# Turning batch 1's q on VectorE instead of TensorE in a fused attention and FFN kernel

## The chip, the cores and the metric

The kernel runs on one core of one Trainium2 chip. The metric is the device time of one execution in microseconds; lower is better. The time before is the median of three runs.

## The reference

Pooled attention over 8 batches, 8 heads, 576 positions and 64 channels per head, then a feed-forward network on the result, all in fp32:

```
k_p, v_p = mean of k, v over groups of 8 positions        # 72 keys per head
attn     = softmax(q k_p^T / 8) v_p                       # [8, 8, 576, 64]
x        = attn as [4608, 512]
h        = x @ w_in                                       # [4608, 2048]
g        = h + sin(alpha h)^2 / alpha
out      = g @ w_out                                      # [4608, 512]
```

## The kernel before

**Two halves.** The first half computes g and writes it to DRAM (`g_bridge`); the second reads it back and multiplies by w_out. Both matrix products are done by Strassen-like schemes with seven products of blocks in place of eight (names such as `a11`, `as1`, `as4` and `bt` are blocks and their sums or differences). The change is in the first half, near its beginning.

**Units and slots.** The first half runs over units u of 512 tokens (`hidden`, from line 839). A unit has four groups J of columns of w_in, and each group seven slots: slot 7J + k holds one block product of four matmuls (`product`, line 863, matmul at line 871), which the trace shows as eight instructions. The products k = 0 to 6 of a group go through four PSUM banks b1, b6, b5, b7; VectorE adds what comes out of them into the tile `h` (line 842), ScalarE takes sines and squares (lines 1056 and 1063), `finish` adds the squares (line 1111), and `store_g` sends the group to DRAM. w_in is loaded in four parts, one for each J (`load_w_in_part`), and each part is combined by four additions (`combine_w_in`, line 692) into the blocks that the seven products need.

**Attention beside the products.** While unit u runs, the attention of batch b = u + 1 is worked out in between: `carry` (line 1233) puts each of its steps into the list of a slot with `at(slot, step, ...)`, and `hidden` calls the list at that slot. The order in which the program issues instructions is the order on each engine; there is no other scheduler, and every queue (SP's DMA queue too) works in that order. The first batch is done before unit 0, in `first_batch`. Unit 0 is the case changed here; there batch 1's attention runs beside the products of unit 0.

The steps of batch 1 are:

- `load_k`, `load_q`, `load_v`: DMAs on SP's queue; GpSimd pools k and v by additions (`pool_rows`, line 132). The tiles `kvin` for k and v are two, used in turn.
- `pairs_q`: ScalarE copies q so that two heads lie side by side (line 98).
- `q_t(i)`: TensorE transposes four pairs of heads of one block of 128 positions (line 294; five blocks, the last with 64 positions), and ScalarE or VectorE copies the result out of PSUM (line 295) to the tile that the scores read.
- `k_t`: TensorE turns the pooled keys (line 283), VectorE copies them (line 284).
- `two_scores(j)`: the scores of two blocks (line 322), with `shifts` on VectorE (lines 345, 346) that take the maximum away; it uses banks 5, 6, 7 and one that the FFN's rotation leaves free.
- `exp` (ScalarE), `norm` (sums on VectorE, the product on GpSimd, line 379), `turn` (VectorE turns blocks of 32x32 of the weights into the tile `tr`, lines 508 to 518), `move` (16 DMAs from `tr` to `aM`, line 528), `all_values` (TensorE, lines 617 and 630), `to_x` (ScalarE writes the next unit's x).

**Batches 2 to 7 already differ from batch 1.** Their q is turned by `turn_q` (line 220): VectorE turns 32x32 blocks into `tr` (lines 233 and 238), and 16 DMAs put the blocks where the scores read them (line 248). `columns` (line 297) and `value_parts` (line 547) know both layouts. Batch 2's q is turned and moved in slots 23 to 26 of unit 0.

**Other lines named below.** Line 837 (`sums_of_x`) is VectorE's difference of blocks of x; line 466 is the norm of batch 0's last 64 rows; line 217 sums batch 0's v, line 1157 is warm-up work before the inputs are there.

Of the kernel before, what the change touches and what calls it, by code (L numbers as in the profile page):

```python
# [19 lines left out]
P = 128  # L20
# [20 lines left out]
class Kernel:  # L41
# [46 lines left out]
    def pairs_q(self, b, tiles):  # L88

        nc = self.nc  # L90
        if 0 in tiles:
            self.raw = self.q_views(self.qm[b])
            self.qm[b] = self.q_tile(1)
        x = self.qm[b][:].rearrange("p (t h e d) -> p t e h d", t=5, e=2, d=self.D)
        for t in tiles:
            n = P if t < 4 else 64
            raw = self.raw[0][:, :, t, :] if t < 4 else self.raw[1]
            nc.scalar.copy(out=x[:n, t], in_=raw.rearrange("p (e h) d -> p e h d", e=2))
# [35 lines left out]
    def load_v(self, b, parts=(0, 1, 2)):  # L134
# [6 lines left out]
        for s in range(2):  # L141
            if s in parts:
                nc.sync.dma_start(out=t[64 * s:64 * s + 64],
                                  in_=self.v[b, 4 * s:4 * s + 4, 0:4 * P, :].rearrange("h (p t) d -> p h (t d)", t=POOL))
# [74 lines left out]

    def turn_q(self, b, part):  # L220
# [42 lines left out]
    def attention(self, b):  # L263
# [22 lines left out]
        def q_t(i, copy=nc.scalar.copy):  # L286

            n = rows[i]
            x = self.qm[b][:n].rearrange("p (t hp x) -> p t hp x", t=5, hp=NP)[:, i]
            if b not in self.qt:  # L290
                self.qt[b] = self.qt_view(self.q_tile(0))
            ps = self.abank([P, NP, P])
            for hp in range(NP):
                nc.tensor.transpose(ps[:, hp, :n], x[:, hp], self.ident[:n, :n])  # L294
            copy(out=self.qt_tiles(b)[:, i, :, :n], in_=ps[:, :, :n])

        def columns(hp, i):

            if b < 2:
# [230 lines left out]
        def to_x(ps, hp, t0, m, s0=0):  # L530

            while s0 < m:
# [5 lines left out]
                if t0 and b > 1:  # L538
# [8 lines left out]
        def value_parts(hp, rest):  # L547
# [14 lines left out]
            order = lambda x: x.rearrange("p a (t i) -> p t a i", i=32) if b == 1 else x  # L562
            at = lambda r, n, h: order(self.aM[r:r + n, :, 128 * h:128 * h + 128])
# [74 lines left out]
        return SimpleNamespace(**{f.__name__: f for f in (k_t, q_t, products, score, two_scores, two_shifts, exp, norm, new_a, turn, move, values, values_rest, all_values,  # L638
# [497 lines left out]
    def first_batch(self):  # L1136
# [96 lines left out]
    def carry(self, u):  # L1233
# [6 lines left out]
        if u == 0:  # L1240
# [509 lines left out]
```

## Time and profile before

| what | us |
|---|---|
| median of three runs | 898.12 (897.59 to 899.59) |
| the profiled execution | 897.74 |
| span of the profiled execution, first to last instruction | 895.9 |
| TensorE busy in it | 890.3 |
| VectorE busy | 682.0 |
| ScalarE busy | 458.7 |
| GpSimd busy | 243.5 |

The profile's times are microseconds from the start of the span. Rows of the chain give start, length and what ran. Rows of the timeline give start, busy time, engine, line, operation, tiles, shapes and count, and in brackets how long the engine was idle before and what ended that. Rows that begin with a line number give minimum, median and maximum duration in ns. SPq is the queue that issues DMAs; a DMA's issue is shown there, not its landing. A row of the table by windows gives the stretch, its length, the busy time (and count) of PE, PEld, DVE, ACT and POOL, TensorE's granted clock, the DMA engines' mean busy share, and GB/s. PE is TensorE, PEld its weight loads, DVE VectorE, ACT ScalarE, POOL GpSimd. Every instruction of an fp32 product appears twice.

### The profile page before, as it was taken

What the parts mean: (1) busy time and instruction counts of PE and PEld (TensorE: products, weight loads), DVE (VectorE), ACT (ScalarE), POOL (GpSimd) and SP (SyncE); (2) the same over time, 40 slices, a digit from 0 to 9 for tenths busy, and PEclk for the clock granted to TensorE, in tenths of its full rate; (3) what the DMA queues carried; (4) which work ended last, traced back from release to release, by engine and by line L of the source; (5) the groups of instructions that cost most, each with busy time, mean ns of one, the idle gap of its engine ahead of it and who ended that gap; (6) DMA issues with size and microseconds to landing.
All of it is one profiled execution on the core that took longest, in us unless ns stands there. A gap on an engine that the chain in (4) does not pass through costs nothing.

```text
span 895.9 us, 16414 instructions
## 1 busy us (share of the span) xinstructions
PE 890.3 (99%) x6310; PEld 814.6 (91%) x6310; DVE 682.0 (76%) x924; ACT 458.7 (51%) x1069; POOL 243.5 (27%) x265
## 2 busy tenths in 40 slices
PE   9999999999999999999999999999999999999998
PEld 6787888888888888888888999999999999999998
DVE  7876767768576675765677889898897896996885
ACT  5687877878878797787776711111111211111111
POOL 6699444624356342524523000000000000000000
PEclk9999999999999999999999999999999999999999
DMA  9958677576765857348126243716435355164002
GB/s 256 252 159 240 193 188 221 154 210 199 188 201 162 229 182 190 131 126 317 54 107 217 104 179 104 231 36 218 117 103 159 92 158 160 36 194 142 18 18 53
DMA packets 119533, 141.03 MB, mean 157 GB/s; under 512 B 45776, under 2 KB 86496, under 8 KB 119456
## 3 DMA queue, kind: packets, MB, share of 16 engines
q1 hardware_dynamic: 116288, 137.39, 52.3%
q10 hardware_dynamic: 3168, 2.61, 1.0%
q8 instruction: 50, 0.82, 0.4%
q14 instruction: 27, 0.22, 0.1%
HBM read 75.37 MB, written 47.19 MB: 137 GB/s over the span
## 4 chain that ended last, share of the span: by engine, by line
PE 98%; DMA 1%; SPq 0%; issue 0%; DVE 0%; ACT 0%
PE PS L871 43%; PE PS L1420 43%; PE PS L1089 6%; PE PS L322 2%; PE PS L617 2%; PE PS L630 1%; DMA h<-in_v_dram 1%; PE PS L575 0%; PE PS L294 0%; PE PS L283 0%; PE PS L573 0%; SPq L169 0%; PE PS L483 0%; PE PS L429 0%; PE PS L217 0%; PE PS L491 0%
## 5 line engine op out<-in xcount | busy, mean ns | idle before, releaser
L871 PE MATMUL PS<-home,a 128*128 128x256 f32 x1072 | 255.7, 381 | 0.1
L871 PEld LDWEIGHTS PS<-home,a 128*128 128x128 f32 x1072 | 197.1, 190 | 29.6 <-issue 4.6
L871 PE MATMUL PS<-home,as 128*128 128x256 f32 x688 | 167.9, 382 | 0.0
L871 PEld LDWEIGHTS PS<-home,as 128*128 128x128 f32 x688 | 124.8, 190 | 16.6 <-ACT PS L843 1.2
L1420 PE MATMUL PS<-s,wb 128*128 128x192 f32 x672 | 116.2, 326 | 0.0
L1063 ACT ACTIVATE s<-s,c 128x256 f32<-128x256 f32 (+1 forms) x236 | 115.5, 556 | 0.0
L1420 PEld LDWEIGHTS PS<-s,wb 128*128 128x128 f32 x672 | 110.4, 190 | 0.1
L842 DVE TENSOR_TENSOR h<-PS,p 128x512 f32<-128x512 f32 x72 | 49.3, 684 | 56.5 <-PE PS L871 34.0
L1591 ACT COPY PS<-PS 128x192 f32<-128x192 f32 x42 | 12.7, 303 | 145.9 <-PE PS L1420 129.7
L1420 PE MATMUL PS<-r,wb 128*128 128x192 f32 x432 | 79.0, 326 | 0.0
L1056 ACT ACTIVATE s<-h,al 128x256 f32<-128x256 f32 x144 | 65.4, 509 | 17.4 <-DVE h L842 13.0
L132 POOL TENSOR_TENSOR kvin<-kvin 96x768 f32<-96x768 f32 (+3 forms) x42 | 69.9, 1665 | 10.1 <-DMA kvin<-in_v_dram 7.3
L1420 PEld LDWEIGHTS PS<-r,wb 128*128 128x128 f32 x432 | 71.7, 190 | 0.0
L1420 PE MATMUL PS<-s,a 128*128 128x192 f32 x384 | 70.3, 326 | 0.0
L1056 ACT ACTIVATE s<-PS,al 128x256 f32<-128x256 f32 x144 | 60.2, 471 | 16.8 <-PE PS L871 16.1
L1420 PEld LDWEIGHTS PS<-s,a 128*128 128x128 f32 x384 | 63.7, 190 | 0.0
L1621 ACT COPY PS<-PS 128x192 f32<-128x192 f32 x42 | 12.7, 303 | 89.8 <-PE PS L1420 89.8
L843 ACT COPY PS<-PS 128x512 f32<-128x512 f32 x72 | 41.6, 578 | 32.8 <-PE PS L871 25.0
L1111 DVE TENSOR_TENSOR h<-PS,s 128x512 f32<-128x512 f32 x36 | 24.8, 688 | 43.1 <-ACT s L1063 43.1
L1359 DVE TENSOR_TENSOR s<-r 128x768 f32<-128x768 f32 x54 | 51.4, 952 | 4.8 <-PE PS L1420 2.8
L379 POOL TENSOR_TENSOR ex<-ex,sm 128x576 f32<-128x576 f32 (+1 forms) x28 | 35.3, 1270 | 72.9 <-DVE sm L378 38.8
L1420 PE MATMUL PS<-s,we 128*128 128x192 f32 x288 | 52.7, 326 | 0.0
(246 smaller groups left out, 1473.0 us busy)
## 6 DMA issues: line engine op xcount, KB each, us to landing
g_bridge<-h SPq DMA_DIRECT2D x72, 512.0 KB
r<-g_bridge SPq DMA_DIRECT2D x15, 1536.0 KB
x<-g_bridge SPq DMA_DIRECT2D x8, 1536.0 KB
out_dram<-o SPq DMA_DIRECT2D x90, 96.0 KB
kvin<-in_k_dram SPq DMA_DIRECT2D x14, 576.0 KB
q<-in_q_dram SPq DMA_DIRECT2D x7, 1024.0 KB
kvin<-in_v_dram SPq DMA_DIRECT2D x14, 512.0 KB
aM<-tr SPq DMA_DIRECT2D x54, 92.0 KB
```

Source lines behind the costliest of these rows:

```text
L132: self.nc.gpsimd.tensor_tensor(out=t[..., 0:w] if w > D else out, in0=t[..., 0:w], in1=t[..., w:2 * w], op=OP.add)
L322: nc.tensor.matmul(ps[e][r0 + r:r0 + r + q.shape[-1], h, :], q[s], kb[s, hp, :], start=True, stop=True)
L379: nc.gpsimd.tensor_tensor(out=E(i), in0=E(i), in1=sm.unsqueeze(2).to_broadcast([P, n, Sp]), op=OP.mult)
L842: add = lambda o, x, y: nc.vector.tensor_tensor(out=o, in0=x, in1=y, op=OP.add)
L843: copy = lambda o, x: nc.scalar.copy(out=o, in_=x)
L871: nc.tensor.matmul(ps[:, jj, :], self.A[p][:, kk, f * P:(f + 1) * P], x[:, kk, :], start=(start and n == 0), stop=(kk == 1), skip_group_ch ...
L1056: self.nc.scalar.activation(out=G.s[:, i, jj, j, :], in_=src[:, jj], func=AF.Sin, scale=self.al[:, f:f + 1])
L1063: self.nc.scalar.activation(out=x, in_=x, func=AF.Square, scale=self.c[:, f:f + 1])
L1089: nc.tensor.matmul(o, W[m][:, G.J - J0], X[m], start=start and n == 0, stop=True, skip_group_check=True)
L1111: add = lambda o, x, y: self.nc.vector.tensor_tensor(out=o, in0=x, in1=y, op=OP.add)
L1359: tt = lambda o, x, y, op: nc.vector.tensor_tensor(out=o, in0=x, in1=y, op=op)
L1420: nc.tensor.matmul(out, W[:, J // 2, J % 2, :], A[:, J, :], start=(start and J == 0), stop=(J == self.NJ - 1), skip_group_check=True)
```

## The change

For batch 1, `pairs_q` and `q_t` are gone. A new `turn_first_q` does for batch 1 what `turn_q` does for the later ones, in six parts: parts 0 and 1 are VectorE's turns of heads 0 to 3 and 4 to 7, part 2 its turn of the last 64 positions, parts 3, 4 and 5 are the 16 moves (6, 6 and 4 DMAs) on SP's queue. q's last rows are loaded in the layout of the later batches, and `columns`, `to_x` and `value_parts` treat batch 1 like these. The first scores go from slot 6 to slot 10, the second from 11 to 12; the key turn from slot 4 to 6; exps, norms and turns of the first two blocks move two or three slots back. On SP's queue, v and w_in's part 3 now follow the moves; v's second half goes to ScalarE's queue; batch 2's q is loaded at slot 13, ahead of its k, not at slot 9. On GpSimd, w_in's part 0 is finished ahead of batch 1's key pooling, part 2 is combined at slot 6 and most of part 3 at slot 10, behind v's main pooling; the rest of v is pooled at slot 17.

```diff
-    def pairs_q(self, b, tiles):
...
     def load_q_rest(self, b, at=None):
-        if b < 2:
-            self.nc.sync.dma_start(out=self.q_views(self.qm[b])[1] if at is None else at, in_=self.q[b, :, 4 * P:, :].rearrange("h p d -> p h d"))
+        if b == 0:
+            self.nc.sync.dma_start(out=at, in_=self.q[b, :, 4 * P:, :].rearrange("h p d -> p h d"))
             return
...
-    def load_v(self, b, parts=(0, 1, 2)):
+    def load_v(self, b, parts=(0, 1, 2), queue=None):
...
-                nc.sync.dma_start(out=t[64 * s:64 * s + 64],
+                (queue or nc.sync).dma_start(out=t[64 * s:64 * s + 64],
...
+    def turn_first_q(self, part):
+
+        nc = self.nc
+        if part == 0:
+            self.tr = self.new_tr()
+            self.qt[1] = self.q_tile(1)[:]
+        tr = self.tr[:, 0:2560].rearrange("p (k x) -> p k x", k=2)
+        if part < 2:
+            x = self.q_views(self.qm[1])[0][:, 4 * part:4 * part + 4].rearrange("p hp t (k i) -> p (hp t) k i", i=32)
+            nc.vector.transpose(out=tr[:, :, 768 * part:768 * part + 512].rearrange("p k (n i) -> p n k i", i=32), in_=x)
+            return
+        if part == 2:
+            nc.vector.transpose(out=tr[:64, :, 512:768].rearrange("p k (n i) -> p n k i", i=32),
+                                in_=self.q_rows(self.qm[1]).rearrange("p (n k i) -> p n k i", k=2, i=32))
+            return
+        for e, a in (((0, 1), (0, 2), (0, 3)), ((1, 0), (0, 0), (1, 1)), ((1, 2), (1, 3)))[part - 3]:
+            w = 768 if a == e else 512
+            to, at = (512, 512) if a == e == 1 else (self.q_at(a), 768 * e)
+            for k in range(2):
+                r = 64 * e + 32 * k
+                nc.sync.dma_start(out=self.qt[1][r:r + 32, to:to + w], in_=tr[32 * a:32 * a + 32, k, at:at + w])
...
-        def q_t(i, copy=nc.scalar.copy):
...
         def columns(hp, i):
 
-            if b < 2:
+            if b == 0:
...
-                if t0 and b > 1:
+                if t0 and b:
...
         self.load_w_in_part(0, ((2, 1, 0),))
+        self.combine_w_in(0, (3,), nc.gpsimd)
         for e in range(2):
             self.load_k(1, e)
             self.pool_k[e]()
-        self.combine_w_in(0, (3,), nc.gpsimd)
         self.load_q(1)
         self.load_w_in_part(1)
...
             at(2, self.sums_of_x, 0, 2)
-            at(2, self.sums_of_x, 0, 3)
             at(2, self.load_w_in_part, 2)
-            at(2, self.load_w_in_part, 3)
-            at(2, self.pairs_q, 1, (0, 1))
-            at(3, self.pairs_q, 1, (2, 3, 4))
+            for r in (32, 96):
+                at(3, self.nc.gpsimd.memset, self.aM[r:r + 32, :, 704:736], 0.0)
             at(4, self.combine_w_in, 1, (0, 1, 2, 3), self.nc.gpsimd)
-            at(4, A.q_t, 0, self.nc.vector.tensor_copy)
-            at(4, A.q_t, 1, self.nc.vector.tensor_copy)
-            at(4, A.k_t)
-            at(7, self.load_v, 1)
-            at(7, lambda: (self.pool_v_main(), self.pool_v()))
+            at(3, self.turn_first_q, 0)
+            at(3, self.turn_first_q, 3)
+            at(3, self.sums_of_x, 0, 3)
+            for part in (1, 2, 4):
+                at(5, self.turn_first_q, part)
+            at(5, self.load_v, 1, (0,))
+            at(5, self.turn_first_q, 5)
+            at(5, self.load_w_in_part, 3)
+            at(9, self.load_v, 1, (1,), self.nc.scalar)
+            at(10, self.load_v, 1, (2,))
+            at(6, A.k_t)
+            at(6, self.combine_w_in, 2, (0, 1, 2, 3), self.nc.gpsimd)
+            at(10, lambda: self.pool_v_main())
+            at(10, self.combine_w_in, 3, (0, 1, 2), self.nc.gpsimd)
             for i in range(2):
-                at((6, 11)[i], A.two_scores, i)
+                at((10, 12)[i], A.two_scores, i)
             at(13, A.two_shifts)
-            for i in range(2, 5):
-                at((8, 8, 9)[i - 2], A.q_t, i)
-            at(9, A0.exp, 4)
-            at(13, A0.norm_rest)
+            at(12, A0.exp, 4)
             for i in range(4):
-                at((9, 9, 15, 15)[i], A.exp, i)
-                at((10, 10, 16, 16)[i], A.norm, i)
-                at((13, 13, 19, 19)[i], A.turn, i)
-            at(8, self.combine_w_in, 2, (0, 1, 2, 3), self.nc.gpsimd)
-            at(17, self.combine_w_in, 3, (0, 1), self.nc.gpsimd)
-            at(17, self.combine_w_in, 3, (2, 3), self.nc.gpsimd)
+                at((12, 12, 15, 15)[i], A.exp, i)
+                at((13, 13, 16, 16)[i], A.norm, i)
+                at((15, 15, 19, 19)[i], A.turn, i)
+            at(14, A0.norm_rest)
+            at(16, self.combine_w_in, 3, (3,), self.nc.gpsimd)
+            at(17, lambda: self.pool_v())
...
-            at(9, self.load_q, 2)
+            at(13, self.load_q, 2)
...
-                at(12, self.load_k, 2, e)
+                at(13, self.load_k, 2, e)
```

More of the change, by code (lines that the diff above doesn't have):

```diff
@@ L284, in k_t @@
             nc.vector.tensor_copy(out=kb[:].rearrange("p hp (x j) -> p j hp x", j=3), in_=ps.rearrange("p j (hp x) -> p j hp x", hp=NP))
-        def q_t(i, copy=nc.scalar.copy):
[L288 to L295, printed above, removed]
         def columns(hp, i):
-            if b < 2:
+            if b == 0:
                 if i == 4:
@@ L561, in value_parts @@
             r = 64 * s + 32 * g
-            order = lambda x: x.rearrange("p a (t i) -> p t a i", i=32) if b == 1 else x
-            at = lambda r, n, h: order(self.aM[r:r + n, :, 128 * h:128 * h + 128])
+            at = lambda r, n, h: self.aM[r:r + n, :, 128 * h:128 * h + 128]
             return ([(vm[64 * s:64 * s + 64, 2 * g + e], at(64 * s, 64, 2 * g + e)) for e in range(2)],
@@ L636, in all_values @@
             to_x(rest, slice(0, 4), 512, 64)
-        return SimpleNamespace(**{f.__name__: f for f in (k_t, q_t, products, score, two_scores, two_shifts, exp, norm, new_a, turn, move, values, values_rest, all_values,
+        return SimpleNamespace(**{f.__name__: f for f in (k_t, products, score, two_scores, two_shifts, exp, norm, new_a, turn, move, values, values_rest, all_values,
                                                           k_head, k_last, q_head, rest_q, products_head, soft_shift, soft_exp, norm_head, norm_rest, a_head, a_rest)})
@@ L1273, in carry @@
+            at(14, A0.norm_rest)
+            at(16, self.combine_w_in, 3, (3,), self.nc.gpsimd)
+            at(17, lambda: self.pool_v())
             at(21, A0.a_rest)
             at(24.5, lambda: A0.values_rest((5, 6, 7, (self.turn + 1) % 5)))
-            for r in (32, 96):
-                at(3, self.nc.gpsimd.memset, self.aM[r:r + 32, :, 704:736], 0.0)
             at(19, A.move, range(3))
```

9 lines of the change are left out of this document (removed).

## The prediction

> **What bounds the kernel now.** I read the page first (shares of the engines and the chain that ended last), then the chain in order of time over the first 100 us, then the rows of VectorE, ScalarE, GpSimd and the SP queue there.
>
> ```profile
> span 895.9 us, 16414 instructions
> PE 890.3 (99%) x6310; PEld 814.6 (91%) x6310; DVE 682.0 (76%) x924; ACT 458.7 (51%) x1069; POOL 243.5 (27%) x265
> PE 98%; DMA 1%; SPq 0%; issue 0%; DVE 0%; ACT 0%
> PE PS L1157 <- DVE full L1634: 1.1, 1, 1.1
> PE PS L217 <- DMA h<-in_v_dram: 0.5, 1, 0.5
> ```
>
> TensorE is the bound: 98% of the chain, and the list of its waits has these two rows only, both from before 12 us. So TensorE work that goes away shortens the kernel by its own length, unless some operand now comes late. In the stretch the change touches, the chain (start, length, what) reads:
>
> ```profile
> 27.89 3.65 PE PS L871 x16
> 31.54 0.87 PE PS L294 x8
> 32.41 0.25 PE PS L283 x3
> 32.66 3.48 PE PS L871 x16
> 36.15 1.16 PE PS L322 x64
> 37.31 3.65 PE PS L871 x16
> 40.96 0.89 PE PS L294 x8
> 41.85 1.73 PE PS L871 x8
> 43.58 0.39 PE PS L294 x4
> 43.97 3.65 PE PS L871 x16
> 47.62 1.46 PE PS L322 x76
> ```
>
> L871 is the FFN product: eight instructions, 1.73 us, make one slot. L294 are the transposes that the change removes, L283 the turn of the pooled keys, L322 the scores of batch 1 (`two_scores`), at slots 6 and 11.
>
> **What is removed.** The L294 rows are 0.87 + 0.89 + 0.39 = 2.15 us, with no cover. The stretch behind the last of them is 3.65 us for two slots where 2 x 1.73 = 3.46 is due, a restart of 0.19 us that may go too: 2.15 to 2.34 us. The copies around them go as well:
>
> ```profile
> L98 ACT COPY q<-q x5: 612/620/621, 30.0 to 33.0; 128x512 f32<-128x512 f32 x4, 64x512 f32<-64x512 f32 x1
> L295 DVE COPY q<-PS x2: 680/686/691, 33.7 to 34.3; 128x512 f32<-128x512 f32 x2
> ```
>
> ScalarE loses 5 x 0.62 = 3.1 us and three copies out of PSUM, VectorE 1.4 us. Neither is on the chain, so I book nothing for them. The products of the scores and of the values keep their number and shapes.
>
> **The new slot times.** Without L294, slots 4 and 5 run from 31.54 to 35.0; slot 6 begins with the key turn (0.25), and slots 6 to 9 end at 35.25 + 4 x 1.73 = 42.2. There, at slot 10, stand the first scores now; two slots with their restart and 1.16 us later, at 47.0, the second (slot 12).
>
> **VectorE.** Batch 2's q is turned in this way already, so the new instructions have rows; the timeline shows what they go between:
>
> ```profile
> L233 DVE STREAM_TRANSPOSE tr<-q x12: 1203/1240/1246, 75.6 to 349.5; 128x1024 f32<-128x1024 f32 x12
> L238 DVE STREAM_TRANSPOSE tr<-q x6: 659/661/662, 77.9 to 350.6; 64x512 f32<-64x512 f32 x6
> 29.70 1.08 DVE L837 TENSOR_TENSOR home<-home 128x512 f32<-128x512 f32 x1
> 30.71 2.31 DVE L837 TENSOR_TENSOR home<-home,home 128x512 f32<-128x512 f32 x1
> 35.32 0.66 DVE L842 TENSOR_TENSOR h<-PS,p 128x512 f32<-128x512 f32 x1
> 29.95 1.14 ACT L98 COPY q<-q 128x512 f32<-128x512 f32 x2 [1.07 <-DMA q<-in_q_dram]
> ```
>
> Two turns of 1.24 and one of 0.66 us are 3.14 added against 1.4 removed. q has landed by 29.95, so turn 0 runs behind the first L837, 30.8 to 32.0. The second L837 follows, 1.08 us if like the first, 2.31 if slowed as here: done at 33.1 to 34.3. Slot 6's product reads it at 35.25: covered. L842 waits for slot 4's product (31.54 + 1.73 = 33.3) and is done at 34.0 to 35.0, still ahead of the product that overwrites its bank at 35.25; this is the thinnest cover, 0.25 us. Behind it turns 1 and 2, 1.9 us, end at 35.9 to 36.9. Queued behind them are L842 of slot 6 and the key copy, which TensorE needs at slot 8 (38.7) and slot 10: both covered.
>
> **The moves.** Sixteen DMAs carry the turned blocks into place. Issue, and the way from issue to landing:
>
> ```profile
> L248 SPq DMA_DIRECT2D q<-tr x96: 507/589/1688, 78.6 to 361.6; - x96
> 78.55 15.23 SPq L248 DMA_DIRECT2D q<-tr x16
> 65.93 7.89 SPq L528 DMA_DIRECT2D aM<-tr x12
> 75.57 2.37 DVE L233 STREAM_TRANSPOSE tr<-q 128x1024 f32<-128x1024 f32 x2 [0.66 <-DMA aM<-tr]
> 17.71 16.17 SPq L686 DMA_DIRECT2D a<-in_moe_w_in_dram x12
> ```
>
> The median issue is 0.589 us; the last of twelve similar moves is issued at 73.82 and its reader starts at 75.57, a landing of 1.75 us. Of the twelve w_in issues of the last row eight remain ahead of the moves (w_in 1 and 2), at the mean of 1.35 us until 28.5, so SP is free when turn 0 ends at 32.0. Six moves take it to 35.6; the next six wait for turns 1 and 2 and end at 39.4 to 40.4, landing at 41.2 to 42.2. The first scores need exactly these twelve, at 42.2: no wait at either end, but no margin at the late one. The other bound is the second row: sixteen moves took 15.23 us there, 0.95 each. At that rate twelve end at 32.0 + 11.4 = 43.4 and land at 45.2: a wait of 3.0 us. Below nothing it cannot go. I take 0, because the 15.23 us hold waits for stores and v loads, while here the queue has only w_in 2 in front. v's first part and the last four moves follow, 5 issues, 43.4 and 45.2 landed, against 47.0.
>
> **v, w_in and GpSimd.** Moved past those DMAs on SP are v's first part, w_in 3 and the rest of v; v's second part goes to ScalarE's queue at slot 9, one issue, where ScalarE has over 3.1 us to spare. Who waits is GpSimd:
>
> ```profile
> 34.32 1.28 SPq L143 DMA_DIRECT2D kvin<-in_v_dram x2
> 45.42 3.71 POOL L132 TENSOR_TENSOR kvin<-kvin 128x1024 f32<-128x1024 f32 x2 [7.26 <-DMA kvin<-in_v_dram]
> 49.22 0.73 POOL L132 TENSOR_TENSOR vm<-kvin 128x256 f32<-128x256 f32 x1
> 52.20 1.27 POOL L692 TENSOR_TENSOR as<-a,a 128x512 f32<-128x512 f32 x1
> 57.24 2.25 POOL L379 TENSOR_TENSOR ex<-ex,sm 128x576 f32<-128x576 f32 x2
> 59.46 1.18 POOL L466 TENSOR_TENSOR last<-ex,sm 64x256 f32<-64x256 f32 x2
> 61.46 2.82 POOL L379 TENSOR_TENSOR ex<-ex,sm 128x576 f32<-128x576 f32 x2 [0.57 <-DVE sm L378]
> 64.56 0.67 DVE L508 STREAM_TRANSPOSE tr<-ex 128x512 f32<-128x512 f32 x1
> 40.00:42.00 2.00, 2.00 (x15) 1.72 (x14) 0.64 (x1) 1.11 (x3) 0.00 (x0) 1.00 1.04 201
> ```
>
> GpSimd idled 7.26 us until v landed. The four combines of w_in 2 (4 x 1.27 = 5.1) move into that gap; w_in 0's last moves ahead of batch 1's key pooling, which still ends near 32.5, before the key turn at 35.0. After v come now its main pooling (4.5, to the end of the 49.22 row), three combines of w_in 3 (3.8), the norms (2.25; 1.18 to the 2.0 up to the next row for the last rows, I take 1.5; 2.82): 14.9 us to the last norm. VectorE's last turn of the attention weights, here at 64.56, is due at 62.4 if all moves up by 2.15. So v must land by 62.4 - 14.9 = 47.5. It is issued near 41; its 1.05 MB (128 rows of 2048 floats) at the 201 GB/s of the window row take 5.2 us: 46.2, in time by 1.3 us. I book 0. The other end is today's way from issue to landing, 45.42 - 34.32 = 11.1 us: 52.1, late by 4.6. It can't gain: the last turn also follows TensorE's own slots.
>
> One place has no room:
>
> ```profile
> 94.48 0.77 PE PS L322 x34
> 95.32 1.00 PE PS L322 x44
> ```
>
> The second scores of batch 2 take 1.84 us here against 1.46 above: 0.38 us of waiting for the moves of batch 2's q, which start behind the aM moves of batch 1. So lateness of that chain is passed on whole. Batch 2's q ahead of its k, four slots later than now, costs nothing on SP: q must wait for the second scores (48.5) and is first turned at 75.57.
>
> **The sum.** 2.15 (to 2.34) saved, 0 + 0 given back. The profiled execution took 897.74 us (its span is 895.9, 1.84 lie around it), which gives 895.6; the median of the runs is 898.12, 0.38 above, which gives 896.0.
>
> [...]
>
> **Rivals.** (1) *The moves are late for the first scores.* For it: the 0.95 us of the 15.23 us row, the window's DMA share of 1.04, the 0.25 us at L842. Against: the median issue of 0.589. At the bound, 3.0 us of wait: 898.12 - 2.15 + 3.0 = 899.0; half of it, 897.5.
>
> (2) *v is late, and the kernel slower.* GpSimd works in order; a late v holds its combines and norms, so VectorE's last turns, the aM moves, batch 2's q moves and its second scores. Every us after 47.5 costs one; from 49.7 on the kernel is slower than before, from 51.5 by over 0.2%. At the bound of 52.1: 898.12 - 2.15 + 4.6 = 900.6. For it: v goes behind twelve moves and shares with w_in 3 (1.05 MB more; both at 201 GB/s take 10.4 us and would end at 51.4). Against: v's first part is ahead of w_in 3 on SP. [...]
>
> (3) *Hidden all the same.* The 2.15 us come back in small waits elsewhere, as the 0.38 us at 95: 898.1. For it: VectorE, GpSimd and SP all shift; against: TensorE shows no other wait behind 12 us.
>
> **Chances.** What a measurement can tell is 0.2%, 1.8 us. Forecast 0.50 (of it 0.06 within 0.2%); rival 1 0.22 (faster 0.02, same 0.12, slower 0.08, with more than one late link); rival 2 0.18 (same 0.05, slower 0.13); rival 3 0.10 (same 0.06, slower 0.04). Sums: faster 0.46, same 0.29, slower 0.25. Range: low 898.12 - 2.34 - 0.38 (the wait at 95 gone) - 0.5 (lowest run under the median) = 894.9; high near the bound of rival 2, 900.2, which leaves about 0.1 on each side. The likeliest case alone: 894.9 to 896.9.
>
> **What would show it.** Right: no L294; L322 in the chain at 42.2 and 47.0 in one piece each; VectorE's 1.24 us turns at 30.8 and 34 to 35; q moves issued at about 0.6 us; v's pooling starts before 47.5; slots 2.15 to 2.34 us earlier from 49 us on. Wrong: L322 at slot 10 broken or late (rival 1), L508 waiting for GpSimd by more than now and a longer wait in batch 2's second scores (rival 2), a product of slots 6 to 9 starting late (L842's cover gone).

## The result and the profile after

The changed kernel takes 900.17 us (median of 22 runs, 898.27 to 904.0) against 898.13 (22 runs) before: a ratio of 1.0029, 95% interval 1.0019 to 1.0039. It is slower by 2.0 us, where 2.1 us of gain were forecast. The runs of the changed kernel differ by granted clock: in 13 of the 22 TensorE kept its clock at 0.999 or 1.0 and their median is 899.04 (898.27 to 901.83); in nine it was granted 0.998 or less, and their median is 903.21 (900.79 to 904.0). The profiled execution is one of two at 0.996 (903.56 us, span 901.8), so what it shows is a dear case; no run of the 13 was traced. The profile of before took 897.74.

The head of the page and two rows of the list of TensorE's waits of the changed kernel (the rows left out are waits before 23 us):

```profile
span 901.8 us, 16395 instructions
PE 890.8 (99%) x6290; PEld 814.5 (90%) x6290; DVE 683.7 (76%) x925; ACT 454.7 (50%) x1061; POOL 243.0 (27%) x265
PE PS L321 <- DMA q<-tr: 4.0, 2, 2.9
PE PS L205 <- DMA h<-in_v_dram: 0.8, 1, 0.8
```

Before, TensorE waited for nothing behind 12 us. Now L321, the scores, waits twice for moves of turned q, 4.0 us in all. The timeline of TensorE shows where (start, length, what, idle before it and what ended that):

```profile
42.89 0.84 PE L321 MATMUL PS<-kblk,q 64*64 64x72 f32 x34
46.64 1.23 PE L321 MATMUL PS<-kblk,q 64*64 64x72 f32 x30 [2.92 <-DMA q<-tr]
47.80 5.99 PE L869 MATMUL PS<-home,a 128*128 128x256 f32 x16
98.95 0.83 PE L321 MATMUL PS<-kblk,q 64*64 64x72 f32 x34
100.89 1.00 PE L321 MATMUL PS<-kblk,q 64*64 64x72 f32 x46 [1.11 <-DMA q<-tr]
```

The first scores of batch 1 begin at 42.89, 0.7 us behind the forecast 42.2 (slot 2 already begins at 28.60, where it began at 27.82 before), and break off after 34 of 64 products for 2.92 us. Then comes something that is no wait: the next sixteen products take 5.99 us, where sixteen take 3.72 at a granted clock of 1.00 (a row of experiment 3). The same stretch in windows (length, TensorE's busy time and instructions, then its weight loads, VectorE, ScalarE, GpSimd; the third number from the end is the granted clock):

```profile
44.00:46.00 2.00, 0.00 (x0) 0.00 (x0) 1.93 (x5) 0.12 (x1) 0.00 (x0) 0.90 1.04 214
46.00:48.00 2.00, 1.36 (x31) 1.25 (x32) 0.29 (x2) 0.00 (x0) 0.00 (x0) 0.50 1.06 211
48.00:50.00 2.00, 2.00 (x5) 1.64 (x6) 1.43 (x2) 0.00 (x0) 0.93 (x1) 0.50 1.12 210
50.00:52.00 2.00, 2.00 (x6) 1.55 (x6) 0.00 (x0) 0.38 (x2) 1.92 (x2) 0.50 1.10 354
52.00:54.00 2.00, 2.00 (x24) 1.47 (x26) 0.12 (x1) 1.98 (x5) 1.92 (x3) 0.89 1.06 408
```

The clock was granted at 0.50 from about 45.6 to 52.4 us, an estimate that takes the 0.90 and 0.89 of the two end windows as part 1.00 and part 0.50. The thirty products behind the wait take 0.72 us at 1.00 (in the trace of experiment 8's first kernel, where they stand alone too); they and the sixteen of L869 lose 0.51 + 2.27 = 2.8 us to it. So in this execution the one wait is paid twice.

What holds the moves? The chain names the piece, and the rows of the two issuing queues and of VectorE stand around it:

```profile
40.25 6.26 DMA q<-tr
31.09 1.23 DVE L217 STREAM_TRANSPOSE tr<-q 128x1024 f32<-128x1024 f32 x1
34.75 1.24 DVE L217 STREAM_TRANSPOSE tr<-q 128x1024 f32<-128x1024 f32 x1
35.91 0.66 DVE L220 STREAM_TRANSPOSE tr<-q 64x512 f32<-64x512 f32 x1
32.47 8.38 SPq L228 DMA_DIRECT2D q<-tr  x12
39.61 0.76 ACTq L131 DMA_DIRECT2D kvin<-in_v_dram  x1
40.94 0.66 SPq L131 DMA_DIRECT2D kvin<-in_v_dram  x1
41.65 2.51 SPq L228 DMA_DIRECT2D q<-tr  x4
```

The turns went as forecast, and the twelve moves were issued by 40.85 (32.47 + 8.38), 0.45 us behind the late end of the forecast. But then 5.8 us passed until their reader went on at 46.64, where the prediction had counted 1.75 from the issue to the reader. (The 6.26 us of the chain's row count from the start of the last issue to the landing.) Shortly before, ScalarE had issued its half of v (39.61). The packets of the DMA queues from 41.5 to 43.5 us (count, MB, share of the 16 engines' time), q10 being ScalarE's queue and q1 SyncE's:

```profile
q10 hardware_dynamic: 203, 0.41, 80.3%
q1 hardware_dynamic: 3, 0.01, 2.3%
```

The half of v is 512 KB, 256 packets of 2 KB; 203 of them moved in these 2 us, and three packets of SyncE's queue, none of these from 42 to 43 us. While v passed, the moves stood.

### The profile page after: what moved, and what is told of

Read it like the earlier page. It is cut to its first block, busy times and chain, and to the rows that moved or that the text cites. A ratio compares the mean times of both kernels' runs of the same rounds, so it can differ in the third digit from the quotient of the medians.

```text
span 901.8 us, 16395 instructions
## 1 busy us (share of the span) xinstructions
PE 890.8 (99%) x6290; PEld 814.5 (90%) x6290; DVE 683.7 (76%) x925; ACT 454.7 (50%) x1061; POOL 243.0 (27%) x265
## 4 chain that ended last, share of the span: by engine, by line
PE 91%; DMA 3%; DVE 2%; SPq 1%; POOL 1%; issue 1%; ACT 0%; DVEq 0%; POOLq 0%; ACTq 0%
PE PS L1420 42%; PE PS L869 38%; PE PS L1087 6%; PE PS L321 2%; PE PS L615 2%; DMA g_bridge<-h 1%; DMA q<-tr 1%; DMA h<-in_v_dram 1%; PE PS L628 1%; POOL kvin L120 1%; SPq L258 1%; SPq L228 0%; POOL vr L120 0%; SPq L157 0%; DVE sm L376 0%
## 5 line engine op out<-in xcount | busy, mean ns | idle before, releaser
L869 PE MATMUL PS<-home,a 128*128 128x256 f32 x1072 | 257.5, 383 | 0.1
L869 PEld LDWEIGHTS PS<-home,a 128*128 128x128 f32 x1072 | 198.9, 192 | 30.3 <-issue 4.5
L869 PE MATMUL PS<-home,as 128*128 128x256 f32 x688 | 167.7, 382 | 0.0
L869 PEld LDWEIGHTS PS<-home,as 128*128 128x128 f32 x688 | 125.0, 190 | 16.6 <-ACT PS L841 1.2
L840 DVE TENSOR_TENSOR h<-PS,p 128x512 f32<-128x512 f32 x72 | 49.2, 683 | 62.0 <-PE PS L869 43.4
L841 ACT COPY PS<-PS 128x512 f32<-128x512 f32 x72 | 41.6, 578 | 34.7 <-PE PS L869 27.1
L1109 DVE TENSOR_TENSOR h<-PS,s 128x512 f32<-128x512 f32 x36 | 24.7, 687 | 45.1 <-ACT s L1061 45.1
```

The lines of the kernel that those rows point to most:

```text
L840: add = lambda o, x, y: nc.vector.tensor_tensor(out=o, in0=x, in1=y, op=OP.add)
L841: copy = lambda o, x: nc.scalar.copy(out=o, in_=x)
L869: nc.tensor.matmul(ps[:, jj, :], self.A[p][:, kk, f * P:(f + 1) * P], x[:, kk, :], start=(start and n == 0), stop=(kk == 1), skip_group_ch ...
L1109: add = lambda o, x, y: self.nc.vector.tensor_tensor(out=o, in0=x, in1=y, op=OP.add)
```

## The experiments

Slots are those of the changed kernel's listing (`at(slot, ...)`); line numbers in fences are those of the kernel that ran. Where nothing else is said, each edit is to the changed kernel.

**1. v's second part later, or earlier.** First, at slot 11, when the first scores are already reading:

```diff
-            at(9, self.load_v, 1, (1,), self.nc.scalar)
-            at(10, lambda: self.pool_v_main())
-            at(10, self.combine_w_in, 3, (0, 1, 2), self.nc.gpsimd)
+            at(11, self.load_v, 1, (1,), self.nc.scalar)
+            at(11, lambda: self.pool_v_main())
+            at(11, self.combine_w_in, 3, (0, 1, 2), self.nc.gpsimd)
```

> Edit: v's second part goes to ScalarE's queue at slot 11 instead of 9 (its pooling with it), so behind the first scores. Theory Q (the DMA packets of v's second part, on ScalarE's queue, run ahead of the last moves of q on SP's queue; TensorE then waits 2.9 us in the first scores, and the granted clock falls to 0.5 behind that wait): the last move lands 1.7 to 2 us after its issue, the first scores wait under 0.5 us, the granted clock stays 1.00, and the time is 895.8 to 897.0 us. Rival S (the moves are late because VectorE's turns and SP's issue end late, whatever v does): the wait stays at 2 to 3 us and the time at 898.3 to 901. Rival L (the loss lies further on, in the attention weights' moves and batch 2's q): the wait goes, the time stays above 898.

905.54 us, ratio 1.0073 (1.0056 to 1.0089). From its timelines:

```profile
42.10 1.23 PE L321 MATMUL PS<-kblk,q 64*64 64x72 f32 x64
48.47 1.99 PE L869 MATMUL PS<-home,as 128*128 128x256 f32 x8
53.83 3.71 POOL L120 TENSOR_TENSOR kvin<-kvin 128x1024 f32<-128x1024 f32 x2 [9.59 <-DMA kvin<-in_v_dram]
63.29 0.71 DVE L507 STREAM_TRANSPOSE tr<-ex 128x512 f32<-128x512 f32 x1 [6.83 <-POOL ex L378]
67.84 0.68 DVE L840 TENSOR_TENSOR h<-PS,p 128x512 f32<-128x512 f32 x1
68.57 3.78 PE L869 MATMUL PS<-home,a 128*128 128x256 f32 x8 [6.02 <-DVE h L840]
```

The second row is the product of slot 12. In the kernel before it stands at:

```profile
50.84 1.89 PE L871 MATMUL PS<-home,as 128*128 128x256 f32 x8
```

It begins 2.37 us earlier, and slot 2 begins at the same time in both (27.81 and 27.82): the 2.15 us of the removed transposes, and the restart of 0.19, are real. With v out of the way the first scores are whole, at 42.10. This fits v as the cause, beside the packets above; by itself one whole execution would not show it, since with v at slot 9 some executions are whole too (experiments 5 and 6). But a wait of 6.02 us came in its place, by a chain one should read from the bottom: TensorE waits for VectorE to take a result out of its PSUM bank, an evacuation (L840); VectorE, which works in order, could not reach it because it stood 6.83 us at the turn of the attention weights (L507); that waited for GpSimd's norms; these stood behind the pooling of v, which landed at 53.8, since ScalarE, in order too, came to issue its load only at 46.25.

At slot 7 instead (only the first line moved, 9 to 7):

> Edit: v's second part on ScalarE's queue at slot 7 instead of 9. In the changed kernel the DMA engines were busy 0.32 to 0.48 of the time from 34 to 40 us, so 512 KB fit in there. Theory Q: its 256 packets are through by about 41 us, before the last moves; the first scores wait 0 to 1 us, clock 1.00, time 895.8 to 897.5 us. Rival S: wait 2 to 3 us, time 898.3 to 901. If packets of ScalarE's queue always push SP's aside, the earlier moves are late instead and the wait is 0.5 to 2 us, time 897 to 899.

900.35 us, 1.0022 (1.0012 to 1.0033). Still two waits at the first scores, 1.40 and 0.56 us, and the clock at 0.84 in the stretch from 43 to 54. The profile puts the first wait down to VectorE's L1109; but in the changed kernel the scores began while L1109 was still running (42.19 to 44.50), so an earlier move is likelier. That an earlier v holds earlier moves is not shown. The twelfth move, at any rate, was again 6.04 us from the start of its issue (39.50) to its landing.

**2. v's second part behind the moves, on their own queue.**

```diff
             at(5, self.turn_first_q, 5)
+            at(5, self.load_v, 1, (1,))
             at(5, self.load_w_in_part, 3)
-            at(9, self.load_v, 1, (1,), self.nc.scalar)
```

> Edit: v's second part on SP's queue, behind the last moves and ahead of w_in's part 3. Same data, same amount, no second queue. Theory Q: the moves keep their place in the one queue, the first scores wait under 0.5 us, the clock stays 1.00, time 895.8 to 897.0 us. Rival S: no difference from the changed kernel, 898.3 to 901 us with a wait of 2 to 3 us.

902.0 us, 1.0039 (1.0024 to 1.0054):

```profile
PE PS L869 <- DVE h L840: 2.3, 1, 2.3
52.01 3.71 POOL L120 TENSOR_TENSOR kvin<-kvin 128x1024 f32<-128x1024 f32 x2 [8.02 <-DMA a<-in_moe_w_in_dram]
60.28 2.26 POOL L378 TENSOR_TENSOR ex<-ex,sm 128x576 f32<-128x576 f32 x2
61.47 0.71 DVE L507 STREAM_TRANSPOSE tr<-ex 128x512 f32<-128x512 f32 x1 [3.07 <-DMA q<-in_q_dram]
```

The first scores are whole (1.23 us at 43.45), the clock of the profiled execution stays at 1.00 (three of the six runs were granted 0.997 or 0.998), and the same chain as in 1 costs 2.3 us: v is pooled at 52.0, three sums of w_in follow, the norms begin at 60.28, and VectorE's turn L507 at 61.47. In brackets the last rows name other loads, the last to come by the profile; that the late norms hold L507 is tested in experiment 7.

**3. TensorE kept busy in the wait.** Thirteen products of constants, 2.97 us (about 2.8 was the author's estimate), ahead of the first scores; they change no output:

```diff
+            at(10, self.fill_slot, 13)
             for i in range(2):
                 at((10, 12)[i], A.two_scores, i)
```

> Edit: 13 extra bf16 matmuls (128x512 of ones, about 2.8 us at full clock) on TensorE ahead of the first scores at slot 10; the rest is the changed kernel. They do no work of the kernel; they only keep TensorE busy while the moves land. Theory G (part of the loss is the granted clock of 0.5 for some 7 us behind the wait, 3.4 us, in those runs where it falls): the wait is filled, the clock stays 1.00 in every run, the spread shrinks to about 1 us, and the time is 898.2 to 899.3 us, below the median of the changed kernel though TensorE does 2.8 us more. Without a clock effect: 900 us or more, with the same spread of 898 to 904.

899.37 us, 1.0013 (1.0004 to 1.0023), below the changed kernel although TensorE does 2.97 us more. The scores that follow are whole:

```profile
45.39 1.23 PE L326 MATMUL PS<-kblk,q 64*64 64x72 f32 x64
46.55 3.72 PE L874 MATMUL PS<-home,a 128*128 128x256 f32 x16
```

L874 is L869 of the other listings: sixteen in 3.72 us, at a clock of 1.00. All twelve runs were granted 0.999 or 1.0, against 13 of 22 of the changed kernel. This speaks for an idle TensorE as what lowers the clock; experiment 8 shows it (0.50 behind a wait of 5.47 us). The time alone would not: it is 0.8 us below the changed kernel, but the two intervals overlap, and the runs still spread over 3.1 us (898.51 to 901.62) where about 1 was expected. Nor does this trace show that there was a wait to fill: its twelfth move was issued 0.43 us behind v's load, as in executions whose scores were whole (experiment 6).

**4. All of v ahead of the moves, on SyncE's queue.**

```diff
             at(2, self.load_w_in_part, 2)
+            at(2, self.load_v, 1, (0, 1))
...
-            at(5, self.load_v, 1, (0,))
-            at(9, self.load_v, 1, (1,), self.nc.scalar)
```

> Edit: both halves of v on SP's queue at slot 2, right behind w_in's part 2 and ahead of all moves of q; nothing of v on ScalarE's queue; the rest is the changed kernel. Theory Q2 (two costs traded by where v is loaded: on ScalarE's queue beside the last moves, it holds these and TensorE waits in the first scores; behind the moves, it holds GpSimd's norms, VectorE's turn of the weights and the product's evacuation queued behind that): with v in the stretch where SP waits for VectorE's turn, both go. v lands near 38 us, its pooling starts behind w_in's part 2 at about 43.5, VectorE's turns of the weights wait under 1 us for GpSimd, the last moves land near 42.3, first scores wait 0 to 0.8 us, clock 1.00, time 895.8 to 897.0 us. Rival P (the plan does not pay even without these waits: batch 2's second scores wait for its moves, and small waits add up): 897.5 to 898.8 us. Rival M (1 MB of v ahead of the moves makes the first six moves late, and the last ones with them): wait 1.5 to 3 us, 898.5 to 901.

902.23 us, 1.004 (1.0027 to 1.0052).

```profile
32.00 14.83 SPq L228 DMA_DIRECT2D q<-tr  x16
PE PS L321 <- DMA q<-tr: 3.2, 3, 1.8
```

Now the sixteen moves are issued at 0.93 us each, the prediction's bound from the 15.23 us row. That row's rate was the rate of moves behind v: here it shows again as soon as v is ahead of them. Of the 3.2 us, 1.76 and 0.40 are waits in the first scores of batch 1, 1.00 is one in batch 2's. To see whether batch 2's moves pay in the same way, the same kernel with batch 2's v (1 MB on SyncE's queue) behind its moves:

```diff
-            at(22, self.load_v, 2, (0, 1))
+            at(27, self.load_v, 2, (0, 1))
```

> Edit: as v_first, and batch 2's v is loaded at slot 27 instead of 22, behind the moves of batch 2's q. Theory Q2: the second scores of batch 2 no longer wait for these moves (0.4 us in the kernel before, 1.1 us in the changed one), 0.4 to 1 us less than v_first, 895.2 to 896.5. If those moves are bound by their issue and VectorE's turns alone, no difference from v_first.

901.34 us, 1.0034 (1.0021 to 1.0048). Batch 2's second scores, broken in every version so far but the one of slot 11, are whole:

```profile
98.59 1.53 PE L321 MATMUL PS<-kblk,q 64*64 64x72 f32 x80
PE PS L615 <- DMA aM<-tr: 1.6, 1, 1.6
```

but here a wait of 1.6 us for the moves of batch 1's weights (aM) stands at L615.

**5. The scores later instead.** v stays; batch 1's scores go a slot back, to 11 and 13:

```diff
-                at((10, 12)[i], A.two_scores, i)
+                at((11, 13)[i], A.two_scores, i)
```

> Edit: the changed kernel with the first scores at slot 11 instead of 10 and the second at 13 instead of 12; v as in the change. Theory Q2: the moves are as late as before, but 1.73 us of product run ahead of the scores, so the wait in them falls from 2 to 3 us to 0 to 1.2 us, the clock seldom falls, and the time is 897.0 to 899.0 us, unless the exps and norms behind it are now late for VectorE's turns (a wait of the product for the evacuation, 0.5 to 1.5 us more). Rival S (the scores' wait is not what costs): 900 us as the changed kernel.

898.52 us, 1.0006 (0.9997 to 1.0016): nothing is lost any more, and nothing is won.

```profile
44.14 1.23 PE L321 MATMUL PS<-kblk,q 64*64 64x72 f32 x64
92.98 0.84 PE L321 MATMUL PS<-kblk,q 64*64 64x72 f32 x34
94.58 0.99 PE L321 MATMUL PS<-kblk,q 64*64 64x72 f32 x46 [0.76 <-DMA q<-tr]
```

One part of the gain goes into batch 2's scores, which wait 0.76 us (0.38 before). What the later slot bought this trace does not show, since its twelfth move was issued 0.42 us behind v's load and may not have been late; but all ten runs kept their clock.

**6. v's second part loaded twice**, to double the suspected load:

```diff
             at(9, self.load_v, 1, (1,), self.nc.scalar)
+            at(9, self.load_v, 1, (1,), self.nc.scalar)
```

> Edit: the changed kernel, and v's second part is loaded twice in a row on ScalarE's queue at slot 9 (the same 512 KB again, to the same place; it changes no result). Theory Q: 256 more packets run ahead of the last moves, some 2 to 2.7 us by the 2.5 us that the first 256 take; the first scores wait 4.5 to 5.5 us instead of 2.9, the clock falls in every run, and the time is 904 to 908 us. If the two queues shared the DMA engines evenly, the moves left (under 64 packets) would be through after the first 64 to 128 packets of v and the second load would change the wait by less than 0.5 us: 900 to 901.

904.04 us, 1.0069 (1.0056 to 1.0083), but not for the reason tested:

```profile
39.08 0.74 ACTq L131 DMA_DIRECT2D kvin<-in_v_dram  x1
45.67 0.72 ACTq L131 DMA_DIRECT2D kvin<-in_v_dram  x1
46.49 0.57 ACT L841 COPY PS<-PS 128x512 f32<-128x512 f32 x1 [4.86 <-DMA kvin<-in_v_dram]
```

The second load writes the same tile, so ScalarE stood until the first had landed: TensorE waited 1.7 us for ScalarE's copy (L841) and 3.6 for VectorE's (L840). The first scores were whole at 42.36 in this execution: SyncE issued its twelfth move at 39.59, 0.5 us behind ScalarE's load of v, where in the changed kernel's profile it was 1.24 us behind (40.85 against 39.61). This fits a race between v and the last moves that half a microsecond decides. The other traces with v at slot 9 fit it as well: in experiment 5 and in the first kernel of experiment 7 the twelfth move was 0.42 us behind v's load, and the first scores are whole; in the first kernel of experiment 8 it was 1.04 behind, and its reader went on 5.5 us after the issue. That this race also makes the two groups of the 22 runs is not shown, with one traced execution of each kernel. As a test of doubled load the run says nothing.

**7. The two good parts together**, scores at 11 and 13 and batch 2's v at slot 27; and, against it, the placement without a wait on paper: v's second part on SyncE's queue as in 2, w_in's group 3 summed behind the norms,

```diff
-            at(10, self.combine_w_in, 3, (0, 1, 2), self.nc.gpsimd)
-            at(16, self.combine_w_in, 3, (3,), self.nc.gpsimd)
+            at(16, self.combine_w_in, 3, (0, 1, 2, 3), self.nc.gpsimd)
```

without and with batch 2's v at 27; and that last edit alone in the kernel before.

> The changed kernel with batch 1's scores one slot later (11 and 13) and batch 2's v loaded at slot 27 and not 22, behind the moves of batch 2's q. With the scores later alone the time was 898.5, and the trace left 0.76 us of waiting for the moves of batch 2's q, which stand behind two loads of v of 512 KB each on SyncE's queue. My theory (each half of v that starts ahead of moves holds them, in batch 2 as in batch 1): the 16 moves take 10.8 us to issue and not 14.6, the second scores of batch 2 are whole (1.53 us), and the time is 897.8. Rival (what is won before 100 us is lost further on, to variations of the feed-forward part): no wait there, but still 898.5. A third: the later v holds batch 2's norms and the time is 899 or more.

> v's second part on SyncE's queue behind the last moves, as in the run that took 902.0, and w_in's group 3 summed behind the norms (slot 16) and not ahead of them (slot 10). In that run GpSimd pooled v at 52.0, then summed w_in for 3.8 us and began the norms at 60.3, and TensorE waited 2.3 us for an evacuation by VectorE that was queued behind the turn of these norms. My theory: norms at about 57, the 2.3 us of waiting gone, the scores of batch 1 whole: 902.0 - 2.3 = 899.7. If the price lies in the sums coming late for their weights or for the pooling of batch 2's k behind them: a new wait at a product or at batch 2's k near 80 us and 901 or more. If v's landing alone sets the norms: no change, 902.

> As the run before it in this set (v's second part on SyncE's queue behind the moves, w_in's group 3 summed behind the norms), with batch 2's v at slot 27 too. This is the placement that takes away all the waits I have found: moves of batch 1 ahead of v, norms ahead of the sums, moves of batch 2 ahead of its v. My theory: another 0.6 to 1.0 below the run without it, 898.9, and no wait for moves left in the trace. Rival (the feed-forward part or the start gives it back): as the run without it, 899.7.

> The kernel before, with batch 2's v loaded at slot 27 and not 22. There the second scores of batch 2 waited 0.38 us for moves behind the two loads of v. My theory: the scores are whole and the time is 0.4 below that of the kernel before, 897.7. Rival: that wait is made up again before the end, 898.1.

| Kernel | us, median (lowest to highest) | ratio to before (898.33) |
|---|---|---|
| scores at 11 and 13, batch 2's v at 27 | 897.49 (895.84 to 900.1) | 0.9994 (0.9985 to 1.0003) |
| v on SyncE's queue, sums behind the norms | 900.27 (898.91 to 901.65) | 1.0023 (1.0013 to 1.0033) |
| the same, batch 2's v at 27 | 899.76 (897.72 to 901.96) | 1.0014 (1.0005 to 1.0024) |
| before, batch 2's v at 27 | 897.87 (897.57 to 898.93) | 0.9996 (0.9987 to 1.0005) |

In the trace of the first row's kernel the sixteen moves of batch 2 took 11.04 us to issue (14.59 in experiment 5), and its second scores are whole. In that of the last row's they took 10.76 us, where the kernel before took 15.23. In each pair only the place of batch 2's v differs: these moves were held by the v ahead of them in their own queue, by 3.55 and 4.47 us.

The second row's kernel did what its edit should: the 2.3 us at L840 are gone, the norms began at 55.23. TensorE's waits are now 1.5 us in batch 2's scores, for its moves, and L615's for aM, 1.6 us:

```profile
PE PS L615 <- DMA aM<-tr: 1.6, 1, 1.6
64.02 10.91 SPq L527 DMA_DIRECT2D aM<-tr  x12
```

Twelve aM moves took 7.89 us to issue before. The list of SyncE's waits has 3.2 us for one of the aM moves themselves here, and no such row in the changed kernel; why stays open. The third row's kernel waits for aM too, 1.3 us. In four runs of the second and four of the third kernel the clock was granted at 0.997 or 0.998; their medians are 901.2 and 901.4, those of the others 899.9 and 898.4.

**8. The best version again, a wait alone, and the edit to before again.** The middle one adds to the best version a 4 KB load on ScalarE's queue and a product that needs it, ahead of the first scores, and nothing else:

```diff
+    def idle(self):
+        t = self.sm.tile([P, 8], F32, name="idle")
+        self.nc.scalar.dma_start(out=t[:], in_=self.q[0, 0, 0:P, 0:8])
+        self.nc.tensor.matmul(self.psum([P, 8], 5), self.ident[:, :P], t[:], start=True, stop=True)
...
+            at(11, self.idle)
```

> The kernel with batch 1's scores at 11 and 13 and batch 2's v at 27 once more, the same code, for its interval: it was at 897.49 against 898.33 of the kernel before. My theory (of the 2.15 us that the removed transposes took, some 0.7 reach the end of the attention stage, since the scores stand a slot later and v's half on ScalarE's queue still brushes the second ones): 897.5 again, 0.6 to 0.9 below the kernel before. Rival (the difference was the draw of the runs): the same time as the kernel before within 0.3 us.

> The kernel of the run beside it with one thing more: ahead of batch 1's first scores TensorE multiplies by a 128x8 tile that ScalarE loads in the same slot (its product goes nowhere), so that it stands idle until those 4 KB land, an estimated 1.5 to 3 us. It leaves the work and the moves as they are and adds a wait alone. Theory that an idle TensorE is paid twice, once as waiting and once as a lower granted clock: the clock falls below 0.9 in the stretch from 43 to 54 us in the profile, and the time rises by the wait and 1.5 to 4 us more. Rival (the wait alone costs): the clock stays at 1.00 and the time rises by the wait, 1.5 to 3 us, no more.

> The kernel before with batch 2's v at 27 once more, the same code, beside the two above on one chip: what of the best kernel's gain is this move of v alone. It was 897.87 against 898.33. Theory: 0.2 to 0.4 below the kernel before, and the best kernel another 0.3 to 0.5 below it. Rival: the same as the kernel before, and the whole gain is that of the removed transposes.

Best version: 897.56 us against 898.13, 0.9996 (0.9986 to 1.0006). The kernel before with batch 2's v at 27: 897.85, 0.9997 (0.9989 to 1.0006). With the wait: 904.71, 1.007 (1.0058 to 1.0083); all its five runs were granted 0.994 to 0.996, where eleven of the best version's twelve kept 0.999 or 1.0. The issue of the small load, TensorE's timeline and windows of the kernel with the wait (the window from 50 to 52, at 0.50 too, is left out):

```profile
45.34 0.36 ACTq L211 DMA_DIRECT2D idle<-in_q_dram  x1
49.90 0.59 PE L212 MATMUL PS<-idle,ident 128*128 128x8 f32 x2 [5.47 <-DMA idle<-in_q_dram]
50.42 2.20 PE L327 MATMUL PS<-kblk,q 64*64 64x72 f32 x64
46.00:48.00 2.00, 0.00 (x0) 0.00 (x0) 0.00 (x0) 1.97 (x3) 0.00 (x0) 0.89 0.92 200
48.00:50.00 2.00, 0.10 (x1) 0.10 (x1) 0.00 (x0) 0.09 (x1) 1.56 (x1) 0.50 1.06 240
52.00:54.00 2.00, 2.00 (x27) 1.59 (x21) 1.93 (x5) 0.45 (x1) 1.92 (x3) 0.50 0.99 380
54.00:56.00 2.00, 2.00 (x10) 1.74 (x9) 1.41 (x3) 1.21 (x3) 1.92 (x3) 0.90 0.35 123
```

The wait was 5.47 us and not the 1.5 to 3 of the author's estimate: ScalarE came to issue the load only 0.9 us into it, and the 4 KB were then 4.5 us on their way. ScalarE's half of v was through by then (no packet of its queue moved from 45 to 46 us), but SyncE's queue, with the other half and w_in, kept the DMA engines busy, 95.8% of their time from 46 to 49 us. The clock fell to 0.50 about 3.1 us into it and stayed there some 6.8 us (the 0.89 and 0.90 of the end windows taken as part 1.00 and part 0.50); the scores took 2.20 us and not 1.23. The time rose by 7.15, by 1.7 more than the wait, 0.5 of it the added product. So in this kernel the idle stretch alone brought the lower clock. What it cost beyond wait and product, 1.2 us, is a little under the 1.5 to 4 expected: 2.3 of the 6.8 us passed while TensorE stood still anyway, and the 0.71 us that the best version's own first scores waited fell away.

## Why the prediction was wrong

**What held.** The removed transposes are worth their 2.15 us at the place where they stood: with no move late, the first scores begin at 42.10 (42.2 forecast) and slot 12 2.37 us earlier than before (experiment 1). VectorE's turns ran at 31.09 and 34.75 and took 1.23 and 1.24 us, the L842 cover (L840 after) held, and the twelve moves were issued by 40.85, within half a microsecond of the late end. The 14.9 us from v's pooling to the last norm were 15.3 in experiment 2 (52.0 to 67.3), and the list of who would wait for a late v was right.

**The step that failed** is the one on the moves: "I take 0, because the 15.23 us hold waits for stores and v loads, while here the queue has only w_in 2 in front". SyncE's queue did have only w_in 2 in front. But the change puts a v load beside it, on ScalarE's queue, and the prediction gave that load a price for ScalarE (one issue) and for GpSimd (its landing) and none for the moves under way on the other queue. No row of the kernel before could have given that price: there only aM moves run on two queues at once (four on ScalarE's, from 65.93). The wait that was taken as 0 measured 2.92 us in the profiled execution. That is very near the 3.0 of the bound, but by another mechanism than the bound's: the issue took 0.70 us a move, not 0.95, and the way from the issue to the reader went from 1.75 to 5.8 us. How the DMA engines choose between the packets of two queues no run here shows. Rival 1 had the place right; its size was right by luck, being worked out from slow issue. That its 899.0 is also the median of the runs that kept their clock (899.04) shows nothing more, since none of these was traced.

**The price left out** is the clock. A wait was booked at its own length everywhere. Experiment 8 shows that a wait alone can bring it down: behind its 5.47 us TensorE was granted 0.50 for some 6.8 us. In the profiled execution the lower clock cost 2.8 us. With the other terms the account of that execution reads: -2.15 (transposes) + 2.92 (wait) + 2.8 (clock) + 0.73 (batch 2's second scores, 1.11 and not 0.38) + 0.8 (slot 2 begins at 28.60 and not 27.82, after longer waits for the first inputs) = 5.1; measured are 903.56 - 897.74 = 5.8. That start varies from one execution to the next (28.11 and 29.06 in the two traces of before with batch 2's v at 27), and 0.7 us are not assigned. In the runs that kept their clock the loss is 0.9 us (899.04 against 898.13).

**v and the norms (rival 2).** v landed at 49.07, 2.9 us behind the estimate of 46.2 and 1.6 behind the 47.5 it was due:

```profile
49.07 3.68 POOL L120 TENSOR_TENSOR kvin<-kvin 128x1024 f32<-128x1024 f32 x2 [5.65 <-DMA kvin<-in_v_dram]
61.61 2.25 POOL L378 TENSOR_TENSOR ex<-ex,sm 128x576 f32<-128x576 f32 x2 [4.25 <-DVE sm L377]
```

It cost nothing in the changed kernel, since its norms waited for VectorE's sums, which came late for TensorE's own reason (the 4.25). Where v was made later still (experiments 1, 2) rival 2 came, and sooner than predicted: not by way of batch 2's moves near 95 us, but directly, by VectorE standing in order at the weights' turn with TensorE's evacuation behind it. The prediction listed the last turn as a point on the way and missed what is queued behind it.

**Batch 2's place without room** was seen rightly. Its 0.38 us were 1.11 after, and they go when that batch's v is put behind its moves.

**What the gain is worth.** With both placements changed, the best version stands at 897.5 in two sets of runs, 0.84 and 0.57 us below the kernel before; neither interval excludes no difference. The kernel before with the v edit alone is 0.46 and 0.28 below. So of the 2.15 us some 0.3 to 0.4 can be ascribed to the removed transposes at the end, and even that is not resolved. Rival 3 (hidden in small waits) describes this version better than the forecast does. The rest can be named only in part. In the repeat's trace the first inputs wait 1.1 us (0.5 before) and the first scores still 0.71; behind batch 2's scores TensorE is 0.64 us ahead of the kernel before (95.68 against 96.32), at the first product of the output stage 0.34 (504.39 against 504.73), and at the last product 0.25 behind (890.90 against 890.65).

## What to carry to other kernels

Price a load for every transfer that is under way on any queue when it starts, and not only for its issuer and its reader: here 512 KB on the idle queue came before a wait of 2.92 us for the busy one. With the reader a slot later nothing was lost; with the load behind the moves the scores were whole, but the wait came back at another place. Price a TensorE wait of some 3 us as the wait plus the lower clock that can follow it: here 2.92 us of wait and 2.8 us at 0.50. And for a late producer, walk the in-order queue of each engine that waits for it: what stands behind the waiting instruction is late too.

## What the runs showed of the hardware

Around the waits of these traces, windows of 2 us give a granted clock of 1.00, of 0.50, or of a value between at the ends of a lower stretch; the lengths and starts here are estimates that take such a value as part 1.00 and part 0.50. Behind waits of 1.76 and 0.40 us (experiment 4: 0.85, 0.50 and 0.80 from 44 to 50 us), of 1.40 and 0.56 (slot 7: 0.52 and 0.63 from 46 to 50) and behind a single one of 2.71 (experiment 4's second kernel: 0.80, 0.50 and 0.84 from 44 to 50) the lower stretch lasted some 3.4 us; behind 2.92 and 5.47 us (the windows above) and 6.02 (experiment 1: 0.53, 0.50, 0.50 and 0.76 from 66 to 74) some 6.8. In these six it began 1.9 to 3.6 us behind the start of the idle stretch. Behind the 3.6 us of experiment 6 the clock was 0.96 from 54 to 100 us, which comes to some 3.7 us at 0.50. In these traces no single wait below 2.7 us brought it, not even the 2.3 us of experiment 2 (1.00 from 54 to 75 us), though two of 1.96 us together did (slot 7): length alone does not decide.

A late wait differs between the traces: the output stage begins with a load of 1.5 MB that VectorE waits for. In the kernel before it was issued at 512.66, in the kernel with v at slot 7 at 515.51, and VectorE went on at:

```profile
520.69 0.96 DVE L1359 TENSOR_TENSOR s<-r 128x768 f32<-128x768 f32 x1 [1.48 <-DMA r<-g_bridge]
525.21 0.96 DVE L1359 TENSOR_TENSOR s<-r 128x768 f32<-128x768 f32 x1 [3.15 <-DMA r<-g_bridge]
```

8.0 and 9.7 us after the issue. TensorE waited for nothing behind it in the one and 1.3 us in the other; in the traces of the other kernels it waited between nothing and 1.3 us. With one trace of each kernel it stays open whether this is chance or follows from the edits. It is as large as what was left to win.
